# Chunked attention and a token/channel mixer on one core: x of one block put by in DRAM, a gate on seven parts, three additions without priority

## The chip, the cores and the metric

The kernel runs on one core of a Trainium2 chip. The metric is the device time of one execution in microseconds (us); the time before is the median of three runs. A profile comes from one further execution, and its times count from the start of that execution's span.

## The reference

Four batches of 768 tokens. A local attention with 8 heads of 64 dimensions gives x (768 x 512 per batch); a mixer adds a low-rank product over the tokens and then a two-layer network over the channels (512 to 2048 to 512).

```python
for c in range(768 // 32):                    # chunks of 32 queries
    k_full = concat(mem_k, k[16 before the chunk .. 8 after it])
    v_full = concat(mem_v, v[the same rows])
    a = softmax(q_c @ k_full.T / 8)
    out[:, :, 32 * c:32 * c + 32] = a @ v_full
x = out as (batch, 768, 512)
u = x + (x.transpose(0, 2, 1) @ U @ V).transpose(0, 2, 1)
result = u + relu(u @ w_ch1) @ w_ch2          # all in float32 accuracy
```

The weights U, V, w_ch1 and w_ch2 arrive as float64 words and are decoded in the kernel.

## The kernel before

To keep float32 accuracy, each float32 operand is split into a high part (fp32r) and a low part, and a product is made of three passes of TensorE (PE): high by high, high by low, low by high. Tokens are worked in blocks of 384 (TB = 3 tiles of 128, so two blocks per batch), hidden channels in 16 factors f of 128 (NF).

**Stages.** `attention(0)` runs first. Then `both_blocks` works off batch 0 in 32 units, numbered n: units 0 to 17 alternate between block 0 and block 1 over f = 0 to 8 while the weights are still being decoded, units 18 to 24 finish block 0 (f = 9 to 15), units 25 to 31 finish block 1. A unit is a `w1_step` (12 matmuls into a bank of PSUM, then ReLU: hh on ACT, hl on VectorE, DVE) and later a `w2_step` (9 matmuls into three accumulator banks). During the last units batch 1's attention is woven in. The attention result x of a token tile is a 128 x 512 tile in SBUF, kept in `xs` in one of 19 equal slots (pool `tk`) until the sums of w2 are added to it in `add_to_x` (L1174). `put_by` hands x to a list, `let_go` issues the listed stores on ACT's queue (or, when told, on SP's), and `recall` gets new slots and loads x back from DRAM on SP's queue.

**The seam.** Batches 1 to 3 use a seven-product scheme (Strassen-like) in place of eight products. For that, three calls of `fold_both` (L1379 to L1399), one for each of the last units of batch 0, transpose x of batch 1 and make seven combinations of it, held as th (high, cast by ACT, L1393) and tl (low, subtracted by DVE, L1394), each with parts 0 to 6. One fold writes its parts in four pieces: 5 and 6, 0 and 1, 2 and 3, and part 4; the planner runs them in the order in which their inputs come, part 4 second. Then `seven` runs `products(p)` for each pair p of factors: seven products of six matmuls (L1459) on three banks; product 0 uses part 6, product 1 part 2, product 2 part 0. After each product, DVE or ACT combines banks (L1465 to L1478).

GpSimd builds five weight sums per pair in `prepare` (L1346). Before those of pair 1, a one-element copy into `gate_` (L1334) reads part 4 of tl at the last token: GpSimd works in program order, so nothing of its later work runs before that element is written.

**What sets the order.** SP, PE and GpSimd follow the program's order. ACT (from unit 2 on) and DVE (from unit 18 on) follow an order that a planner makes ahead of time from its own estimates: it takes the ready instruction of the highest priority. Priority is program order, and `tc.high_priority(offset=...)` lifts an instruction by so many places; HIGH is 400. The fold is lifted by HIGH, so are the combinations in `products`, and the last additions to x by 2 x HIGH.

Of the kernel before, what the change touches and what calls it, by code (L numbers as in the profile page):

```python
# [9 lines left out]
F32 = mybir.dt.float32  # L10
# [26 lines left out]
HIGH = 400  # L37
LEAD = 0
LATE = 0
SPLIT = 9  # L40
# [15 lines left out]
def chunk_attn_then_mixer_kernel(  # L56
# [13 lines left out]
    nc = tc.nc  # L70
    ctx.enter_context(tc.manual_schedule(engines={mybir.EngineType.SP}))
    P = 128
# [16 lines left out]
    TB = 3  # L89
    NBLK = NT // TB  # L90
    TOK = TB * P
# [3 lines left out]
    const = ctx.enter_context(tc.tile_pool(name="const", bufs=1))  # L95
# [13 lines left out]
    def slot(shape, dtype, name):  # L109
        return tk.tile(shape, dtype, name=name, tag="slot")  # L110
# [58 lines left out]
    for j in range(4):  # L169
        nc.gpsimd.tensor_copy(  # L170
            out=rep[32 * j:32 * j + 32],
            in_=ident[32 * j:32 * j + 32, None, 32 * j:32 * j + 32].broadcast_to([32, 3, 32]),
# [242 lines left out]
    def advance(n):  # L415
        for _ in range(n):
            next(weights, None)
# [652 lines left out]
    def more_w():  # L1070
        while loaded[0] < min(NF, done[0] // 2 + EARLY):
            if loaded[0] >= 5 and front[0]:
                return
            if loaded[0] >= LASTF - NDEC and done[0] < ndec[0]:
                return
            load_w(loaded[0])
            loaded[0] += 1
# [26 lines left out]
    rest, gate = [], []  # L1104

    def turn_x1(c):

        ps = att_ps()
        for tt in range(TB):
            nc.tensor.matmul(  # L1110
                out=ps[:, tt * P:(tt + 1) * P], lhsT=xs[(0, TB + tt)][:, c * P:(c + 1) * P],
                rhs=ident, start=(tt == 0), stop=False, is_transpose=True, skip_group_check=True,
            )
        return ps
# [8 lines left out]
    def join_uT1(ps, c, g3):  # L1123
        if (0, 1) not in uT:
            u_pair(0, 1)
        uh, ul = (a[c] for a in uT[(0, 1)])
        nc.tensor.matmul(
            out=ps[:, 0:TOK], lhsT=g3[:, c * P:(c + 1) * P], rhs=v3[:, TOK:2 * TOK],
            start=False, stop=True, skip_group_check=True,
        )  # L1130
        nc.scalar.copy(out=uh, in_=ps[:, 0:TOK])  # L1131
        nc.vector.tensor_tensor(out=ul, in0=ps[:, 0:TOK], in1=uh.bitcast(F32), op=ALU.subtract)
# [5 lines left out]
    def put_by(b, t):  # L1138
        held.append((x_d[b, t], xs.pop((b, t))))

    def let_go(eng=nc.scalar):
        while held:
            to, x = held.pop(0)
            eng.dma_start(out=to, in_=x)

    def recall(b, blk):
        for t in range(blk * TB, blk * TB + TB):
            x = xs[b, t] = slot([P, CH], F32, "x")
            nc.sync.dma_start(out=x, in_=x_d[b, t])
# [20 lines left out]

    def add_to_x(b, t, bank, last):
        x = xs[(b, t)]
        with tc.high_priority(offset=2 * HIGH if last else 0):
            nc.vector.tensor_tensor(out=x, in0=bank, in1=x, op=ALU.add)  # L1174
        if last:
            held.append((out[b, t * P:(t + 1) * P, :], xs.pop((b, t))))
            if b == B - 1 or b == 0 and t >= TB:
                let_go(nc.sync)
        else:
            put_by(b, t)  # L1180
# [42 lines left out]
    def get_w1l(f):  # L1223
        if f not in w1ls:
            w1ls[f] = fetch_w1l(f)

    def both_blocks(following):

        units = []
        for f in range(SPLIT + LEAD):  # L1230
            if f < SPLIT:
                units.append((0, f, 0, f == 0, None))
            if f >= LEAD:
                g = f - LEAD
                units.append((1, g, 1, g == 0, False if g == SPLIT - 1 else None))
        units += [(0, f, 0, False, True if f == NF - 1 else None) for f in range(SPLIT, NF)]
        units += [(1, f, 0, f == SPLIT, True if f == NF - 1 else None) for f in range(SPLIT, NF)]
        prev = []
        for n, (blk, f, where, begins, ends) in enumerate(units):
            while done[0] < min(2 * NF, 2 * f + 1 + (n > LATE)):  # L1240
                advance(1)
                more_w()
            if n == 2:
                head.close()
            let_go()
            solo = n >= 2 * SPLIT
            if n == 2 * SPLIT:
                paced.close()
            for blk_, m, *_ in units[n:n + AHEAD + 1]:
                if m >= SPLIT and blk_ == 1:  # L1250
                    get_w1l(m)
            w1l = w1ls[f]
            if f >= SPLIT or blk == 1:
                del w1ls[f]
            if n == 2 * SPLIT - SOON:
                place(1)
            serve(RATEL if n < 2 * SPLIT else RATES)
            if n > 2 * SPLIT:
                border()
            if n == 0:  # L1260
                for c, g3 in rest[:2]:
                    join_uT1(turn_x1(c), c, g3)
            if n == len(units) - 1:
                for m in range(3):
                    build_factor(0, m)
            hid_ = w1_step(0, blk, f, w1l)
            if n == len(units) - 5:
                open_turned()
            if n == len(units) - 1:
                open_fast()  # L1270
            if n == 0:
                decode(2, 4)
                for c, g3 in rest[2:]:
                    join_uT1(turn_x1(c), c, g3)
                decode(1, 1)
                decode(2, 6)
                decode(1, 6)
                decode(3, 2)
            for _ in range(RATE + (3 < n < 12)):
                advance(1)  # L1280
                more_w()
            if n > 2 * SPLIT:
                border()
            if n == len(units) - 3:
                prepare(0, True)
            if n >= len(units) - 3:
                following()
            if n == len(units) - 1:
                recall(0, 1)
                for m in (3, 4):  # L1290
                    build_factor(0, m)
            prev.append((blk, f, where, begins, ends) + hid_)
            if solo or n % 2 == 0 or ends:
                while len(prev) > (not ends):
                    while done[0] < 2 * prev[0][1] + 2:
                        advance(1)
                        more_w()
                    w2_step(0, *prev.pop(0))

    def place(n):  # L1300
        for _ in range(n):
            next(gen[0], None)

    def serve(n):
        for _ in range(n):
            if next(feed[0], "shut") == "shut":
                return
# [10 lines left out]
    def border():  # L1318
        run_tails()
        place(PLAN[at[0]])  # L1320
        at[0] += 1

    gate_ = const.tile([P, 1], F32, name="gate")
    sums_d = [[dram.tile([P, 2, 2, P], F32, name=f"sumsd{p}_{m}") for m in range(3)] for p in range(NF // 2)]

    def prepare(p, first):

        if first:
            whole = [slot([P, NCK, P], F32, "val") for _ in range(2)]
            for side in range(2):  # L1330
                nc.gpsimd.dma_start(out=whole[side], in_=val_d[2 * p + side])
            mixed[p, 1], mixed[p, 3] = whole[1][:, 2:4, :], whole[0][:, 0:2, :]
            if p == 1:
                nc.gpsimd.tensor_copy(out=gate_[0:1], in_=turned[0][1][0:1, 4, 0, TOK - 1:TOK].bitcast(F32))  # L1334
        else:
            plain = slot([P, 2, 2, P], F32, "plain")
        for m, (n, fa, ca, fb, cb, op) in enumerate(SUMS):
            if m % 2 == 0:
                two = slot([P, 2, 2, P], F32, "sums")
                used = slice(0, 1 if m + 1 == len(SUMS) else 2)  # L1340
                if not first:
                    nc.sync.dma_start(out=two[:, used], in_=sums_d[p][m // 2][:, used])
            mixed[p, n] = two[:, m % 2]
            if first:
                a, b_ = (whole[f][:, 2 * c:2 * c + 2, :] for f, c in ((fa, ca), (fb, cb)))
                nc.gpsimd.tensor_tensor(out=two[:, m % 2], in0=a, in1=b_, op=getattr(ALU, op))  # L1346
                if m % 2 == 1 or m + 1 == len(SUMS):
                    summed.append((p, sums_d[p][m // 2][:, used], two[:, used]))
            elif m == 0:
                for n, side in ((1, 1), (3, 0)):  # L1350
                    mixed[p, n] = plain[:, side]
                    nc.sync.dma_start(out=plain[:, side], in_=val_d[2 * p + side][:, 2 * side:2 * side + 2])
# [9 lines left out]
    turned = [None]  # L1362
# [234 lines left out]
```

## Time and profile before

| | us |
|---|---|
| median of three runs | 647.34 |
| the three runs | 647.22, 647.34, 649.98 |
| the profiled execution | 647.76 |
| its span, first to last instruction | 646.0 |
| TensorE busy in the span | 626.6 (97%) |
| VectorE busy | 422.4 (65%) |
| ScalarE busy | 306.6 (47%) |
| GpSimd busy | 75.0 (12%) |

PE, DVE, ACT, POOL and SP are TensorE, VectorE, ScalarE, GpSimd and SyncE. Matmuls are pipelined and overlap in the records, so PE's progress is read from starts, not from sums of durations. A wait is put down to the instruction whose signal came last. A DMA issue is shown at the engine whose queue issues it (ACTq, SPq); where the queue stands, everything behind it in that engine's program stands too.

### The profile page before, as it was taken

The numbers are of one execution on the slowest core, as the hardware profiler recorded it, in microseconds if no ns is written. First come the engines' busy times: TensorE is split into PE (matmuls) and PEld (weight loads), VectorE is DVE, ScalarE is ACT, GpSimd is POOL, SyncE is SP. The second block draws the span as 40 slices with busy tenths as digits, with TensorE's granted clock in tenths as the row PEclk, the third lists the DMA queues.
The fourth block names the chain that finished last, engine by engine and source line by source line (L and its number), as shares of the span: only waits on it lengthen the run. The fifth ranks groups of instructions, "written<-read, shape, count | busy, mean of one in ns | idle before, by whom it ended". The sixth has DMA issues, their size and how long they took to land.

```text
span 646.0 us, 15746 instructions
## 1 busy us (share of the span) xinstructions
PE 626.6 (97%) x6196; PEld 548.8 (85%) x6198; DVE 422.4 (65%) x889; ACT 306.6 (47%) x770; POOL 75.0 (12%) x129
## 2 busy tenths in 40 slices
PE   7798999999999999989999999999999999999997
PEld 6567999988879899879898899888888899889986
DVE  4977997887529867449676864556666974427442
ACT  4666776685316454524344555633333653315320
POOL 3710011100120642123300000000000000000000
PEclk9999999999999999989999999999999999999999
DMA  9998695696606689414371699144532662100021
GB/s 206 192 306 294 212 261 180 181 255 177 185 22 220 183 219 208 132 35 157 100 236 52 170 208 230 43 116 124 148 114 82 189 221 90 50 34 16 2 79 69
DMA packets 134357, 96.83 MB, mean 150 GB/s; under 512 B 88842, under 2 KB 111114, under 8 KB 134282
## 3 DMA queue, kind: packets, MB, share of 16 engines
q1 hardware_dynamic: 121690, 70.25, 41.2%
q10 hardware_dynamic: 9936, 17.04, 7.2%
q0 software_dynamic: 2656, 8.52, 3.8%
q8 instruction: 49, 0.80, 0.5%
q14 instruction: 26, 0.21, 0.1%
HBM read 69.44 MB, written 25.43 MB: 147 GB/s over the span
## 4 chain that ended last, share of the span: by engine, by line
PE 88%; DVE 4%; SPq 2%; ACT 2%; DMA 2%; issue 1%; DVEq 0%; ACTq 0%
PE ps_h L1459 19%; PE acc L1213 14%; PE ps_h L1159 10%; PE ps_a L1459 8%; PE acc L1218 7%; PE ps_h L1213 6%; PE ps_a L1213 5%; PE ps_h L1218 3%; PE ps_a L582 2%; PE ps_a L1218 2%; PE ps_a L790 2%; PE ps_a L661 2%; PE ps_h L1205 1%; PE ps_a L760 1%; PE ps_a L1379 1%
## 5 line engine op out<-in xcount | busy, mean ns | idle before, releaser
L1213 PE MATMUL acc<-w,hh 128*128 128x512 f32 x366 | 97.1, 400 | 0.9 <-DVE w L367 0.9
L1459 PE MATMUL ps_h<-th,w1l 128*128 128x384 f32 x288 | 83.3, 342 | 0.5 <-DVE part L1474 0.5
L1213 PEld LDWEIGHTS acc<-w,hh 128*128 128x128 f32 x366 | 66.9, 188 | 15.2 <-issue 1.5
L1435 DVE SCALAR_TENSOR_TENSOR hl<-kept,hh 128x384 fp32r<-128x384 f32 x48 | 26.7, 556 | 50.9 <-PE ps_a L1218 25.7
L1459 PEld LDWEIGHTS ps_h<-th,w1l 128*128 128x128 f32 x288 | 52.8, 187 | 3.7 <-issue 1.7
L1434 ACT ACTIVATE hh<-kept 128x384 fp32r<-128x384 f32 x48 | 25.5, 531 | 64.0 <-PE ps_a L1213 41.5
L1459 PE MATMUL ps_h<-th,s 128*128 128x384 f32 x192 | 53.0, 337 | 0.0
L1218 PE MATMUL acc<-w,hl 128*128 128x512 f32 x183 | 51.6, 390 | 0.0
L1459 PE MATMUL ps_h<-tl,w1l 128*128 128x384 f32 x144 | 48.5, 337 | 0.0
L1213 PE MATMUL ps_h<-w,hh 128*128 128x512 f32 x156 | 43.9, 404 | 1.8 <-issue 1.8
L1159 PE MATMUL ps_h<-uh,w1h 128*128 128x384 f32 x124 | 42.5, 348 | 0.7 <-ACT uh L1131 0.6
L1159 PE MATMUL ps_h<-ul,w1h 128*128 128x384 f32 x124 | 40.9, 337 | 0.0
L1218 PEld LDWEIGHTS acc<-w,hl 128*128 128x128 f32 x183 | 34.4, 188 | 7.4
L1213 PE MATMUL ps_a<-w,hh 128*128 128x512 f32 x132 | 38.1, 392 | 1.7 <-ACT hh L1165 1.7
L1465 ACT COPY part<-ps_h 128x384 f32<-128x384 f32 x24 | 11.5, 479 | 55.5 <-PE ps_h L1459 34.5
L1427 ACT CAST s<-sums 128x256 fp32r<-128x256 f32 x72 | 28.6, 411 | 16.3 <-PE ps_h L1459 16.1
L1213 PEld LDWEIGHTS ps_h<-w,hh 128*128 128x128 f32 x156 | 29.0, 192 | 7.8 <-issue 1.9
L1459 PEld LDWEIGHTS ps_h<-th,s 128*128 128x128 f32 x192 | 35.1, 188 | 0.2 <-DVE part L1469 0.2
L1346 POOL TENSOR_TENSOR sums<-val 128x256 f32<-128x256 f32 x40 | 31.9, 825 | 28.1 <-DMA val<-vald 11.0
L1459 PE MATMUL ps_h<-tl,s 128*128 128x384 f32 x96 | 32.3, 337 | 0.0
L1213 PEld LDWEIGHTS ps_a<-w,hh 128*128 128x128 f32 x132 | 25.0, 190 | 7.5 <-ACT hh L1165 2.2
L1428 DVE TENSOR_TENSOR s<-sums,s 128x256 fp32r<-128x256 f32 x72 | 30.4, 434 | 1.0 <-ACT s L1427 0.8
(280 smaller groups left out, 1393.8 us busy)
## 6 DMA issues: line engine op xcount, KB each, us to landing
sums<-sumsd SPq DMA_DIRECT2D x32, 256.0 KB
xd<-x ACTq DMA_DIRECT2D x30, 256.0 KB
x<-xd SPq DMA_DIRECT2D x30, 256.0 KB
rw<-in_moe_w_ch_dram SPq DMA_DIRECT2D x14, 512.0 KB
vb<-in_v_dram SPq DMA_DIRECT2D x56, 98.0 KB
raw<-in_moe_w_ch_dram SPq DMA_DIRECT2D x20, 256.0 KB
qn<-in_q_dram SPq DMA_DIRECT2D x36, 128.0 KB
rw<-in_moe_w_ch_dram SPq DMA_DIRECT2D x16, 256.0 KB
```

Of the source, the lines that this page charges most:

```text
L582: nc.tensor.transpose(out=psv[:, p, r, :], in_=half[:, r, 2 * p:2 * p + 2, :].rearrange("n h d -> n (h d)"), identity=ident,)
L661: nc.tensor.matmul(out=psv[s][CK * i:CK * i + CK, t, p % 2, p // 2, :], lhsT=qt[p // 2][rows, p % 2, NI * t + i, :], rhs=kall[rows, NB * ( ...
L790: nc.tensor.matmul(out=psv[g][CK * i:CK * i + CK, t, j], lhsT=pt[j % 2][rows, 2 * t + j // 2, CK * i:CK * i + CK], rhs=vt[rows, NI * t + i ...
L1159: nc.tensor.matmul(out=ph[:, :TOK], lhsT=w[:, c, :], rhs=u[c], start=(m == 0), stop=(m + 1 == len(parts)),)
L1213: nc.tensor.matmul(out=acc[tt], lhsT=h[:, sl], rhs=w, start=(begins and m == 0), stop=False,)
L1218: nc.tensor.matmul(out=acc[tt], lhsT=hl[:, sl], rhs=w2h[f], start=False, stop=ends is not None)
L1346: nc.gpsimd.tensor_tensor(out=two[:, m % 2], in0=a, in1=b_, op=getattr(ALU, op))
L1427: nc.scalar.copy(out=s[:, 0:2], in_=total)
L1428: nc.vector.tensor_tensor(out=s[:, 2:4], in0=total, in1=s[:, 0:2].bitcast(F32), op=ALU.subtract)
L1434: nc.scalar.activation(out=hh, in_=src, func=AF.Relu)
L1435: nc.vector.scalar_tensor_tensor(out=hl, in0=src, scalar=0.0, in1=hh.bitcast(F32), op0=ALU.max, op1=ALU.subtract,)
L1459: nc.tensor.matmul(out=banks[at_], lhsT=w[:, wc, :], rhs=t[:, i, c, :], start=(n < 3 and m == 0), stop=(m + 1 == len(parts)), skip_group_c ...
```

## The change

At unit 2 of `both_blocks` the three x tiles of batch 0's block 0 are put by: stored to DRAM on ACT's queue and their slots given back. At unit 21 (2 x SPLIT + 3, SPLIT = 9) they are recalled on SP's queue into three new slots; the additions to them come after unit 24. The gate copies one element of each of tl's seven parts, not of part 4 alone. The last additions of batch 0's block 1 (t of 3 and more) keep the place that the program gives them; the other last additions keep their lift of 2 x HIGH.

```diff
     def add_to_x(b, t, bank, last):
         x = xs[(b, t)]
-        with tc.high_priority(offset=2 * HIGH if last else 0):
+        with tc.high_priority(offset=2 * HIGH if last and (b > 0 or t < TB) else 0):
             nc.vector.tensor_tensor(out=x, in0=bank, in1=x, op=ALU.add)
...
             if n == 2:
                 head.close()
+                for t in range(TB):
+                    put_by(0, t)
+            if n == 2 * SPLIT + 3:
+                recall(0, 0)
             let_go()
...
-    gate_ = const.tile([P, 1], F32, name="gate")
+    gate_ = const.tile([P, 7], F32, name="gate")
...
             if p == 1:
-                nc.gpsimd.tensor_copy(out=gate_[0:1], in_=turned[0][1][0:1, 4, 0, TOK - 1:TOK].bitcast(F32))
+                nc.gpsimd.tensor_copy(out=gate_[0:1], in_=turned[0][1][0:1, :, 0, TOK - 1].bitcast(F32))
```

## Rows read from the trace of the kernel before

**Rows 1.** Waits of PE, 50 to 216 us: us in total, times, longest.

```profile
PE ps_a L1213 <- ACT hh L1165: 1.7, 1, 1.7
PE ps_a L661 <- issue: 1.1, 1, 1.1
PE ps_a L1459 <- DVE tl L1394: 1.0, 1, 1.0
PE acc L1213 <- DVE w L367: 0.9, 1, 0.9
```

**Rows 2.** Timeline of PE at the seam: start us, us, operation [idle before].

```profile
213.56 0.34 PE L1459 MATMUL ps_a<-th,w1l 128*128 128x384 f32 x1
214.91 0.44 PE L1459 MATMUL ps_a<-tl,w1l 128*128 128x384 f32 x1 [1.02 <-DVE tl L1394]
...
215.90 0.34 PE L1459 MATMUL ps_h<-th,w1l 128*128 128x384 f32 x1
```

**Rows 3.** Windows, two pairs: us, busy of each engine, clock, DMA.

```profile
212.49:221.26 8.77, 7.75 (x44) 7.29 (x42) 7.94 (x15) 3.64 (x10) 6.46 (x10) 1.00 0.65 212
221.26:228.58 7.32, 7.32 (x43) 7.29 (x43) 4.50 (x11) 2.28 (x5) 5.53 (x9) 1.00 0.79 169
```

**Rows 4.** Timeline of DVE at the seam, columns as in group 2.

```profile
211.63 1.02 DVE L1394 TENSOR_TENSOR tl<-fold,th 128x512 fp32r<-128x512 f32 x2
212.56 1.28 DVE L1174 TENSOR_TENSOR x<-acc,x 128x512 f32<-128x512 f32 x2
213.76 2.23 DVE L1394 TENSOR_TENSOR tl<-fold,th 128x512 fp32r<-128x512 f32 x2
215.92 0.68 DVE L1174 TENSOR_TENSOR x<-acc,x 128x512 f32<-128x512 f32 x1
```

**Rows 5.** Timeline of GpSimd (POOL) at the seam.

```profile
212.71 0.18 POOL L1334 COPY gate<-tl 1x1 f32<-1x1 f32 x1 [7.77 <-DVE tl L1394]
212.89 4.63 POOL L1346 TENSOR_TENSOR sums<-val 128x256 f32<-128x256 f32 x5
```

**Rows 6.** DVE's groups by form, 199 to 208 us: busy us, mean ns, idle.

```profile
L1394 DVE TENSOR_TENSOR tl<-fold,th 128x512 fp32r<-128x512 f32 x6 | 3.9, 686 | 0.0
```

**Rows 7.** DVE's groups by form, 212.6 to 217 us.

```profile
L1394 DVE TENSOR_TENSOR tl<-fold,th 128x512 fp32r<-128x512 f32 x2 | 2.2, 1155 | 0.0
L1174 DVE TENSOR_TENSOR x<-acc,x 128x512 f32<-128x512 f32 x3 | 2.0, 681 | 0.0
...
L1428 DVE TENSOR_TENSOR w1l<-sums,w1l 128x256 fp32r<-128x256 f32 x1 | 0.4, 409 | 0.0
```

**Rows 8.** Timelines of SP, DVE and PE behind the seam.

```profile
217.05 0.39 SPq L488 DMA_DIRECT2D kn<-in_k_dram  x1
...
221.22 0.38 SPq L491 DMA_DIRECT2D kn<-in_k_dram  x1
...
227.22 0.56 DVE L1435 SCALAR_TENSOR_TENSOR hl<-ps_a,hh 128x384 fp32r<-128x384 f32 x1 [2.06 <-ACT hh L1434]
...
228.58 1.04 PE L582 MATMUL ps_a<-ident,kn 128*128 128x128 f32 x8
```

**Rows 9.** DMA issues, 40 to 235 us: KB, median us to landing.

```profile
val<-vald POOLq DMA_DIRECT2D x8, 256.0 KB, 4.1
```

**Rows 10.** Window around PE's third wait, columns as in group 3.

```profile
130.00:140.00 10.00, 8.93 (x69) 7.75 (x67) 8.62 (x17) 10.00 (x36) 0.00 (x0) 1.00 1.12 294
```

**Rows 11.** Waits of ACT, whole span, columns as in group 1.

```profile
ACT part L1465 <- DMA xd<-x: 17.6, 4, 4.7
```

**Rows 12.** Timelines of DVE and PE beside the new stores.

```profile
62.89 0.69 DVE L367 TENSOR_TENSOR w1l<-vbe,w1h 128x512 fp32r<-128x512 f32 x1
...
64.57 0.87 PE L1159 MATMUL ps_h<-uh,w1l 128*128 128x384 f32 x4
```

**Rows 13.** Timelines of DVE and PE at block 0's last additions.

```profile
167.75 1.89 DVE L1174 TENSOR_TENSOR x<-acc,x 128x512 f32<-128x512 f32 x3 [3.18 <-PE acc L1218]
...
175.93 1.42 PE L1213 MATMUL acc<-w,hh 128*128 128x512 f32 x5
```

## The prediction

> **What bounds the kernel now.** TensorE (PE) does, nearly everywhere, so I looked for the moments at which it stands still. The first view is the list of PE's waits over the part of the span that the change touches, from 50 to 216 us. It names four, 4.7 us together [rows 1]: 1.7 us on ACT's hh, 0.9 us on a low half of w2, 1.1 us that the profile puts down to "issue", and 1.0 us on a DVE subtraction of the fold (tl, L1394). That sum caps what the three edits can give back here. The second view is PE's timeline around 212 us, the seam at which batch 0 ends and batch 1's seven-product scheme begins. Product 1's first matmul starts at 213.56, its second waits 1.02 us for tl, and product 2 starts only at 215.90 [rows 2]. The third view prices the seam as a whole: the first pair of factors takes 8.77 us, the next pair, with the same 42 matmuls, 7.32 us at the same granted clock of 1.00 [rows 3]. The reader is to see that the seam loses 8.77 - 7.32 = 1.45 us, more than the 1.02 us that the wait names, because PE also runs unevenly as it resumes.
>
> The fourth view says why. On DVE, two of the last fold's four tl subtractions run from 211.63, then two additions L1174 of batch 0's result (212.56, 1.28 us for both), then the other two tl from 213.76, which take 2.23 us, then the third addition at 215.92 [rows 4]. GpSimd opens its gate at 212.71, when part 4 of tl is written but parts 0 to 3 are not, and starts its five sums at 212.89 [rows 5]. A tl of this shape takes 686 ns in the two folds before, where GpSimd adds nothing, and 1155 ns here [rows 6, 7]. So PE's wait has two causes: two additions stand ahead of the tl that it needs, and that tl is slow beside GpSimd.
>
> **The change part by part.** *Additions without priority, gate on all parts.* These remove the wait together. Without the 2 x HIGH lift, the three additions rank behind the fold, which keeps its own lift of HIGH. Then the third tl (parts 2 and 3) starts at 212.56, where the first addition stood, and runs 0.69 us, since the gate is shut: it ends at 213.25. In the two folds before, DVE had no idle time ahead of any tl [rows 6], so ACT's casts should not hold it up. PE needs these parts with product 1's second matmul, one matmul interval (1.05 us / 6 = 0.17 us; 7.32 / 7 = 1.05 us per product [rows 3]) after 213.56: at 213.73. That is 0.48 us of room. The fourth tl (parts 0 and 1) ends by 213.25 + 0.69 = 213.94, and PE wants it in product 2, from 213.56 + 1.05 = 214.61. Product 1 shrinks from 215.90 - 213.56 = 2.34 us to 1.05 us, a gain of 1.29 us [rows 2, 3]; the other 0.16 us of the 1.45 is the uneven resumption, which I expect mostly to go too.
>
> What is late next? The additions now start near 213.9 and, at 0.68 us each [rows 7], end near 216.0, against 216.60 before [rows 4]: no later for SP, whose stores of the result wait for them and hold batch 2's loads of k behind them. They could delay the combination L1467, which product 4 needs at 212.49 + 4 x 1.05 = 216.69. L1467 can start when product 1 is done (214.61); if all three additions go first it ends near 216.0 + 0.55 = 216.55. The cost is nothing, by 0.1 us, and at most some tenths.
>
> The gate is a wait, so what is queued behind it on GpSimd counts: five sums for pair 1, two memsets, and the loads of pair 2's values. All start about 1.2 us later than now (213.94 against 212.7). Pair 1's first sum is needed by product 0 of that pair, at 221.26 - 1.45 = 219.8; sums that begin at 214.2 and take 4.63 us for all five [rows 5] end at 218.8. So their delay is covered by the seven products of pair 0. Uncovered, it would cost up to 1.2 us.
>
> The slowdown does not vanish with the gate: it moves to whatever DVE runs beside the sums. The rows show that it spares what would stand there: the additions took 681 ns beside GpSimd, and an L1428 of w1l 409 ns [rows 7]. The Trainium skill (SBUF — State Buffer, "Who interferes with whom") says that a DVE instruction with two SBUF inputs contends with a GpSimd instruction that reads SBUF, and that whoever issues first holds the port pair for the whole instruction. The tl's 686 against 1155 ns agrees; the L1428 at 409 ns, also with two SBUF inputs, shows no cost. By the rule each later L1428 could still wait out a sum.
>
> *x of block 0 to DRAM and back.* It adds three stores on ACT's queue at unit 2 and three loads on SP at unit 21, and frees three of the 19 slots in between. No PE wait between them names a slot or a load, so I book no gain. The cost: the stores' issue can hold ACT, which is in order. The trace has no such store at that place; its bounds are nothing (hidden in idle time) and 4.7 us, the longest hold of ACT by a DMA in this kernel [rows 11]. The tightest work behind is factor 2's low half: DVE writes it at 62.89 + 0.69 = 63.58, and PE wants it at 64.57, so 1.0 us of hold is free [rows 12] and the bounds on the time are 0 and 3.7 us. I take 0, since ACT's waits between 44 and 216 us name no DMA. SP's three loads are needed by the additions that begin at 167.75 and last 1.89 us; PE uses those banks again at 175.93 [rows 13], so the loads may be 6.3 us late before PE notices. Slots are no scarcer after unit 21 than before the change. I book 0 there, too.
>
> **Sum.** -1.29 - 0.16 + 0 = -1.4 us. The profiled run took 647.76 us for a span of 646.0, so 1.76 us lies around the span and stays. It becomes 646.4; taken from the median of 647.34, 645.9 us.
>
> **The rivals.**
>
> *The stall shrinks but stays, or moves.* If the planner, which orders DVE by its own estimates, finds tl not ready when PE's last sums are, it still puts two additions first. Then the closed gate alone helps: tl runs from 213.76 to 214.45 and PE resumes some 0.7 us late instead of 1.3. Or L1467 and the L1428 copies queue up behind additions and sums, by the port rule above. Either gives back 0.4 to 0.9 us of the 1.45: about 646.7. For it: DVE is busy 7.94 of 8.77 us there [rows 3]. Against: the rows of the additions and of L1428 show no slowdown [rows 7].
>
> *A second wait goes, too.* The 1.1 us wait at the first scores of batch 1 [rows 1] falls into a stretch in which ACT is 10.00 of 10 us busy [rows 10]; so it is probably ACT's copy of q, late in its queue. With other slots, the planner may order that stretch otherwise: 645.9 - 1.1 = 644.8. Nothing in the change aims at it.
>
> *Slower: the stores hold ACT at unit 2.* Place: ACT's queue ahead of the casts of factors 1 and 2. It decides from a hold of 1.0 us on; at 4.7 us it costs 3.7 us [rows 11, 12], so 645.9 + 3.7 = 649.6, above the time before. Against: all other ACT waits in this stretch are for DVE or PE.
>
> *Slower still: the additions slide.* With no lift at all they rank behind everything that products raises by HIGH. If the third ran only in DVE's next long gap, 2.06 us ahead of 227.22, SP's loads of k for batch 2 would start there instead of at 217.05. The last of the first group is issued at 221.22 + 0.38 and would land, at the 4.1 us of a 256 KB load, at 225.7; PE transposes at 228.58, or 227.1 after the gain [rows 8, 9]. So the additions may end 1.4 us later than 216.60; each us beyond costs PE one. An end near 224 gives 645.9 + 6 = 652. Against: DVE has nothing else to do at 213.9.
>
> **How the numbers follow.** Forecast 645.9 (own range 645.6 to 646.4): 0.57. Shrunken or moved stall, 646.7: 0.20. Second wait, 644.8: 0.10. Stores hold ACT, up to 649.6: 0.07. Additions slide, about 652: 0.06. The range takes the first three and the lower half of the fourth, with some tenths for the spread of medians: 644.4 to 648.4. A difference below 0.5% (3.2 us) can't be told from no change by such a measurement. Faster than 644.1 would need more waits than the rows name near the edits: 0.04. Slower than 650.6 takes the last rival: 0.06. Same: 0.90.
>
> **What would show it.** In the changed kernel's trace the four tl of the last fold stand in one row near 2.2 us with no addition among them, the gate follows the last of them, the additions come next, and the wait of product 1 for L1394 is gone; the first pair of factors takes about 7.4 us. GpSimd's sums start near 214.2, relative to the seam. Stores and loads of x appear near unit 2 and unit 21 with no new wait of PE. I am wrong if the first pair still takes over 8 us, if a wait for L1467, L1469 or kn replaces the old one, or if a stretch before 205 us has grown.

## The result, and the profile after

The changed kernel is slower, not faster: 651.72 us median of 19 runs (651.1 to 655.63), beside 648.46 us (646.13 to 652.54, 19 runs) for the kernel before in the same session. The ratio is 1.0053 with a 95% interval of 1.0036 to 1.0071. The forecast was 645.9 us, with a range that ended at 648.4. The profiled execution took 652.4 us with a span of 650.6 us, 4.6 us longer than the 646.0 us before.

Where it went is seen best if the start of one and the same matmul is read in both traces (of each kernel one execution):

| matmul of PE | before, us | after, us | later by |
|---|---|---|---|
| scores L661 of batch 0, the group at 25.58 us | 25.58 | 32.28 | 6.70 |
| join of the low-rank product, L1095 | 42.03 | 49.37 | 7.34 |
| a w1 unit, L1159 | 61.38 | 70.09 | 8.71 |
| product 1, second matmul | 214.91 | 223.16 | 8.25 |
| scores of batch 2, L661 | 274.47 | 282.56 | 8.09 |
| w2 step behind the scores of batch 2, L1213 | 277.74 | 284.45 | 6.71 |
| the same stretch, L1213 | 282.28 | 287.55 | 5.27 |
| end of the span | 646.0 | 650.6 | 4.6 |

So the loss is made before 33 us, ahead of every stretch that the prediction looked at. At the seam the change gains, but some 0.5 us instead of 1.45. Between 274 and 283 us the profiled execution of before lost 2.8 us (8.09 - 5.27) that this one did not; that stretch is taken up again below.

The 6.70 us are not all the change's. The profiled execution of before is early in the front part: the kernels below that have no hold there start this L661 group at 26.92 to 28.91 us, 1.3 to 3.3 us behind it, and those with the hold at 32.28 to 32.93. At the first w1 matmul of the unit near 61 us, the start is 61.03 in before, 62.25 to 64.54 in the six kernels without the hold, and 68.53 to 69.45 in the three with it. Between the middles of the last two groups, 62.81 and 68.89, lie some 6 us; that is my estimate of what the hold costs PE by there.

**The loss.** The longest of PE's waits of the changed kernel from 0 to 45 us (total, times, longest); it was 0.6 us before. Behind it the L661 group, in the changed kernel and then in the one before:

```profile
PE ps_a L661 <- ACT qt L642: 6.4, 2, 6.2
...
32.28 2.23 PE L661 MATMUL ps_a<-kall,qt 64*32 64x64 f32 x127 [6.23 <-ACT qt L642]
```

```profile
25.58 1.81 PE L661 MATMUL ps_a<-kall,qt 64*32 64x64 f32 x128
```

ACT's timeline there says why the copies of q (qt, L642) are late:

```profile
25.66 0.44 ACT L216 ACTIVATE dec<-vraw 96x256 f32<-96x256 f32 x1 [0.65 <-DMA vb<-in_v_dram]
31.46 0.34 ACTq L1144 DMA_DIRECT2D xd<-x  x1
31.84 0.39 ACT L642 COPY qt<-ps_h 128x256 f32<-128x256 f32 x1 [5.75 <-DMA vbe<-in_v_dram]
31.94 0.36 ACTq L1144 DMA_DIRECT2D xd<-x  x1
32.11 0.68 ACT L642 COPY qt<-ps_h 128x256 f32<-128x256 f32 x2
```

In the kernel before the same place reads:

```profile
24.74 0.45 ACT L216 ACTIVATE dec<-vraw 96x256 f32<-96x256 f32 x1 [0.79 <-DMA vraw<-in_moe_V_dram]
25.09 1.21 ACT L642 COPY qt<-ps_h 128x256 f32<-128x256 f32 x4
```

The store of x (L1144) belongs to unit 2, which runs after 60 us, but x is ready near 25 us, and the planner has put the store into ACT's queue at once, between the decay factors and the q copies. There ACT stands for 5.75 us, the store's own issue of 0.34 us included. It doesn't wait for x: the bracket names a load of v. In the kernel as built this store carries two waits, one for VectorE and one for a completion counter (number 0 of eight that the DMAs of SP and ACT take in turn); the transfer that used that counter last is this load of v. No run gives the store another counter, so this step rests on the built kernel and the trace. The chain of waits shows when the load came (start us, us, what):

```profile
18.59 6.01 DMA uarea<-in_moe_U_dram
24.60 0.02 issue
24.61 0.61 SPq L563
...
27.04 0.41 SPq L563
...
27.49 0.45 SPq L563
...
27.98 3.41 DMA vbe<-in_v_dram
...
31.41 0.02 ACTq L1144
```

SP's queue was issuing one load after another, and it had itself stood 1.1 us, to 24.60, for an earlier load (uarea); the turn of this load of v came at 27.98, after ACT had already stopped at its store, and it landed 3.41 us later. The Trainium skill (DMA: Bandwidth & Descriptors, "Issuing engines are not separate DMA queues") says that issuing from several engines saves only the time of initiating, which is usually small beside the transfer. One issue of 0.41 to 0.45 us beside the 3.41 us from issue to landing agrees. Ahead of this load stands a row of eight issues that took 5.30 us on the one queue, the stand of 1.1 us among them; so the row, not the single issue, made it late.

While PE stood, its granted clock fell. Windows of the changed kernel, and below them one of the kernel before (us, busy of PE, PEld, DVE, ACT, POOL, granted clock, DMA share, GB/s):

```profile
25.00:30.00 5.00, 1.05 (x10) 0.81 (x8) 2.01 (x7) 0.44 (x2) 0.77 (x2) 0.92 0.87 185
30.00:35.00 5.00, 2.72 (x174) 2.66 (x174) 0.66 (x2) 2.77 (x8) 0.24 (x1) 0.50 0.85 224
35.00:40.00 5.00, 2.99 (x115) 2.06 (x101) 4.60 (x15) 1.26 (x2) 3.28 (x7) 0.89 0.12 34
...
65.00:70.00 5.00, 3.95 (x11) 3.21 (x12) 3.90 (x7) 3.70 (x9) 0.00 (x0) 0.68 0.61 210
```

```profile
30.00:35.00 5.00, 5.00 (x106) 3.12 (x102) 4.70 (x16) 3.19 (x7) 2.96 (x6) 0.66 0.65 148
```

A clock of 0.50 is the level of 1.2 GHz. The L661 group took 2.23 us there (32.28, 127 matmuls) against 1.81 us in before (25.58, 128). The last row of the changed kernel is a second dip, in which the lag grows from 7.34 to 8.71 us; the kernel with the stores alone, below, has the hold but a clock of 1.00 in that window, so I don't count this step to the change.

**The seam.** DVE, GpSimd and PE of the changed kernel, beside [rows 2, 4, 5]:

```profile
220.28 1.02 DVE L1398 TENSOR_TENSOR tl<-fold,th 128x512 fp32r<-128x512 f32 x2
221.22 1.28 DVE L1174 TENSOR_TENSOR x<-acc,x 128x512 f32<-128x512 f32 x2
222.41 1.29 DVE L1398 TENSOR_TENSOR tl<-fold,th 128x512 fp32r<-128x512 f32 x2
223.62 0.69 DVE L1174 TENSOR_TENSOR x<-acc,x 128x512 f32<-128x512 f32 x1
...
223.77 0.18 POOL L1338 COPY gate<-tl 1x7 f32<-1x7 f32 x1 [10.17 <-DVE tl L1398]
...
223.16 0.45 PE L1463 MATMUL ps_a<-tl,w1l 128*128 128x384 f32 x1 [0.60 <-DVE tl L1398]
```

The two additions still stand ahead of the tl that PE needs: the order of [rows 4] is unchanged. The gate now opens after the last tl, and with GpSimd silent these two tl take 1.29 us instead of 2.23. PE's wait for them falls from 1.02 to 0.60 us, and the first pair of factors takes 8.24 us instead of the 8.77 of [rows 3]:

```profile
221.15:229.39 8.24, 7.64 (x43) 7.31 (x42) 7.70 (x14) 3.89 (x11) 5.42 (x10) 1.00 0.64 207
```

The slowdown beside GpSimd has not gone; it has moved to the low halves of the factors, which took 408 to 457 ns behind the seam in before, where the sums were done or nearly so (DVE's groups by form, 223.8 to 229.4 us: busy us, mean ns):

```profile
L1432 DVE TENSOR_TENSOR w1l<-sums,w1l 128x256 fp32r<-128x256 f32 x2 | 1.5, 733 | 0.2 <-ACT w1l L1431 0.2
L1432 DVE TENSOR_TENSOR w1l<-val,w1l 128x256 fp32r<-128x256 f32 x2 | 1.4, 722 | 0.0
```

No wait of PE follows from that here.

### The profile page after: what moved, and what is told of

It reads as the page before. It is cut to its first block, busy times and chain, and to the rows that moved or that the text cites. A ratio compares the mean times of both kernels' runs of the same rounds, so it can differ in the third digit from the quotient of the medians.

```text
span 650.6 us, 15769 instructions
## 1 busy us (share of the span) xinstructions
PE 625.1 (96%) x6198; PEld 548.5 (84%) x6198; DVE 420.7 (65%) x889; ACT 306.1 (47%) x770; POOL 74.4 (11%) x129
## 4 chain that ended last, share of the span: by engine, by line
PE 86%; DMA 4%; DVE 3%; SPq 3%; ACT 1%; issue 1%; ACTq 0%; DVEq 0%
PE ps_h L1463 19%; PE acc L1213 14%; PE ps_h L1159 10%; PE ps_a L1463 7%; PE acc L1218 7%; PE ps_h L1213 6%; PE ps_a L1213 5%; PE ps_h L1218 3%; PE ps_a L1218 3%; PE ps_a L582 2%; DMA rw<-in_moe_w_ch_dram 2%; PE ps_a L661 2%; PE ps_a L790 2%; SPq L563 1%; PE ps_h L1205 1%
## 5 line engine op out<-in xcount | busy, mean ns | idle before, releaser
L1213 PE MATMUL acc<-w,hh 128*128 128x512 f32 x366 | 97.1, 400 | 1.0 <-DVE w L367 1.0
L1213 PEld LDWEIGHTS acc<-w,hh 128*128 128x128 f32 x366 | 66.9, 188 | 15.1 <-issue 1.5
L1213 PE MATMUL ps_h<-w,hh 128*128 128x512 f32 x156 | 43.0, 398 | 0.4 <-issue 0.4
L1159 PE MATMUL ps_h<-uh,w1h 128*128 128x384 f32 x124 | 42.6, 349 | 0.8 <-ACT uh L1131 0.8
L1159 PE MATMUL ps_h<-ul,w1h 128*128 128x384 f32 x124 | 41.1, 339 | 0.0
L1213 PE MATMUL ps_a<-w,hh 128*128 128x512 f32 x132 | 38.6, 396 | 1.7 <-ACT hh L1165 1.7
L1469 ACT COPY part<-ps_h 128x384 f32<-128x384 f32 x24 | 11.5, 479 | 55.7 <-PE ps_h L1463 39.3
L1213 PEld LDWEIGHTS ps_h<-w,hh 128*128 128x128 f32 x156 | 28.4, 188 | 6.2 <-issue 0.6
L1471 DVE TENSOR_TENSOR part<-ps_a,part 128x384 f32<-128x384 f32 x24 | 13.3, 555 | 28.6 <-PE ps_a L1463 26.3
L1213 PEld LDWEIGHTS ps_a<-w,hh 128*128 128x128 f32 x132 | 25.0, 190 | 7.4 <-ACT hh L1165 2.2
```

The costliest lines, as they stand in the source:

```text
L1159: nc.tensor.matmul(out=ph[:, :TOK], lhsT=w[:, c, :], rhs=u[c], start=(m == 0), stop=(m + 1 == len(parts)),)
L1213: nc.tensor.matmul(out=acc[tt], lhsT=h[:, sl], rhs=w, start=(begins and m == 0), stop=False,)
L1471: nc.vector.tensor_tensor(out=ta, in0=b2, in1=ta, op=ALU.subtract)
```

## The experiments

The theory from these rows: the loss is the hold of ACT by the first store, at the place that the planner chose. The rivals: the bytes of six added transfers cost time wherever they run; or the seam, with gate and priority, loses it. The kernels below are the changed kernel with the edit shown, and each is compared with the kernel before in five rounds of the same session.

### The stores and the recall alone

```diff
-        with tc.high_priority(offset=2 * HIGH if last and (b > 0 or t < TB) else 0):
+        with tc.high_priority(offset=2 * HIGH if last else 0):
...
-    gate_ = const.tile([P, 7], F32, name="gate")
+    gate_ = const.tile([P, 1], F32, name="gate")
...
-                nc.gpsimd.tensor_copy(out=gate_[0:1], in_=turned[0][1][0:1, :, 0, TOK - 1].bitcast(F32))
+                nc.gpsimd.tensor_copy(out=gate_[0:1], in_=turned[0][1][0:1, 4, 0, TOK - 1:TOK].bitcast(F32))
```

> The change without its gate and its priority: only the stores of block 0's x at unit 2 and their recall. Hold theory (the planner puts the first store on ACT ahead of the copies of q in batch 0's attention, where it stands 5.75 us for a load of v): all of the loss is here, so 3.3 to 4.5 us above the kernel before, the 6.2 us wait of PE for L642 near 26 us stays, and the seam wait of 1.0 us for tl is back. Rival, seam theory (the gate or the slide of the additions costs): equal to the kernel before within 1 us, no wait of PE above 2 us before 45 us.

Measured: 654.91 us (653.02 to 656.74, 6 runs), ratio 1.0093 [1.0058, 1.0129]. ACT's wait and PE's two waits of interest:

```profile
31.98 0.38 ACT L642 COPY qt<-ps_h 128x256 f32<-128x256 f32 x1 [5.90 <-DMA vbe<-in_v_dram]
...
PE ps_a L661 <- ACT qt L642: 6.8, 2, 6.4
...
PE ps_a L1463 <- DVE tl L1398: 1.0, 1, 1.0
```

The hold is there, and the wait at the seam is back at 1.0 us. The loss comes with the stores. It is larger than I had expected: 6.3 us by the medians, against 3.3 to 4.5. The changed kernel loses 3.3 us in its own session; the gain at the seam explains some 0.5 us of that difference, the two intervals overlap, and the rest stays open.

### The gate and the priority alone

```diff
             if n == 2:
                 head.close()
-                for t in range(TB):
-                    put_by(0, t)
-            if n == 2 * SPLIT + 3:
-                recall(0, 0)
```

> The change without the stores and the recall: only the gate on seven parts and the additions without priority. Hold theory: nothing of the loss, 0.4 to 1.0 us below the kernel before, PE's wait for tl at the seam 0.6 us instead of 1.0, no new wait before 45 us. Seam theory: 3 us or more above the kernel before.

Measured: 646.1 us (644.75 to 651.77, 12 runs) beside 648.62, ratio 0.9968 [0.9943, 0.9993]. This beats both kernels. At the seam:

```profile
213.94 1.01 DVE L1394 TENSOR_TENSOR tl<-fold,th 128x512 fp32r<-128x512 f32 x2
214.88 1.28 DVE L1174 TENSOR_TENSOR x<-acc,x 128x512 f32<-128x512 f32 x2
216.08 1.28 DVE L1394 TENSOR_TENSOR tl<-fold,th 128x512 fp32r<-128x512 f32 x2
...
214.81:222.99 8.18, 7.58 (x44) 7.26 (x43) 7.70 (x14) 3.88 (x11) 5.38 (x10) 1.00 0.64 207
```

The pair takes 8.18 us, 0.59 us less than in [rows 3]. The medians differ by 2.5 us, more than the 0.4 to 1.0 that I had expected; what lies beyond the 0.59 us is open (see the next section).

### The gate alone

```diff
-        with tc.high_priority(offset=2 * HIGH if last and (b > 0 or t < TB) else 0):
+        with tc.high_priority(offset=2 * HIGH if last else 0):
...
-                for t in range(TB):
-                    put_by(0, t)
-            if n == 2 * SPLIT + 3:
-                recall(0, 0)
```

> GpSimd's gate waits for all seven parts of tl; no stores, and the priority of the last additions as in before. VectorE's order near the end of the fold is that of before: tl, tl, addition, addition, tl, tl, addition. If GpSimd's sums beside tl are what the change gained at the seam, the gate alone gives it: the last two tl take 1.28 us in place of 2.23, TensorE's wait for tl falls from 1.0 to 0.6 us, the shift there is -0.4 to -0.5 us, and the time is before -0.4 to -0.6 (the stretch at 276 to 283 us can give up to 1.3 more). If the priority made it, the wait stays at 1.0 and the time at that of before.

Measured: 646.87 us (645.74 to 650.36, 12 runs) beside 648.05, ratio 0.9981 [0.9961, 1.0001]. The two tl again take 1.28 us behind two additions, and PE waits 0.60 us:

```profile
215.85 0.45 PE L1459 MATMUL ps_a<-tl,w1l 128*128 128x384 f32 x1 [0.60 <-DVE tl L1394]
```

As built, this kernel has, on each of the five engines, the same instructions with the same waits in the same order as the kernel of gate and priority above. Likewise, a kernel with the priority edit alone is, instruction for instruction, the kernel before. So the priority edit does nothing at all, and the gain at the seam is the gate's. The two sections thus time one and the same program twice, 2.5 us and 1.2 us below the kernel before: part of the 2.5 us is spread of the medians, and the interval of the second just reaches 1.

### The whole change, stores issued by SP

```diff
                 for t in range(TB):
                     put_by(0, t)
+                let_go(nc.sync)
```

> The whole change, but the three stores are issued on SP, which follows the program's order, at unit 2. Hold theory: ACT meets no store early, PE's 6.2 us wait is gone, the time is 0.5 us below the kernel before to 0.5 above. Traffic rival (768 KB more to move while weights and v stream in, whichever engine issues them): still 2 to 4 us above the kernel before, with waits of ACT or DVE for loads between 45 and 75 us.

Measured: 647.41 us (645.24 to 650.79, 12 runs) beside 648.62, ratio 0.998 [0.9955, 1.0004]. SP follows the program's order, so the stores stay at unit 2:

```profile
L1144 SPq DMA_DIRECT2D xd<-x x3: 319/320/343, 53.9 to 56.1; - x3
```

Of PE's waits for L642 0.2 us are left. The same bytes, stored and recalled at the place that the program names, cost nothing that can be measured beside the kernel before: the rival of the traffic, with 2 to 4 us, falls. Beside gate and priority alone, in the same session, the median is 1.3 us longer, and the intervals overlap.

### The whole change, stores by ACT in the program's order

```diff
             if n == 2:
-                head.close()
                 for t in range(TB):
                     put_by(0, t)
+                let_go()
+                head.close()
```

> The whole change, but put_by and the stores stand ahead of head.close, so ACT still follows the program's order and the stores come behind unit 1's casts. Hold theory: no hold near 26 us; at their new place the stores wait for loads already under way, up to 1.4 us each by SP's waits there, of which about 1 us is free: 0.5 us below the kernel before to 2 us above. Traffic rival: 2 to 4 us above, as in the kernel with the stores on SP.

Measured: 650.53 us (647.67 to 653.92, 12 runs) beside 648.62, ratio 1.0024 [0.9999, 1.0048]. The stores now stand at 64 us, behind a cast of w, and hold nothing there; PE doesn't wait for qt at 26 us. What is left comes from elsewhere. Waits of PE, and ACT's timeline at the longer one:

```profile
PE ps_a L661 <- issue: 5.1, 2, 3.6
...
142.43 0.71 ACT L391 CAST w2last<-vb 128x512 fp32r<-128x512 f32 x1
142.94 0.53 ACT L216 ACTIVATE dec<-rw 128x256 f32<-128x256 f32 x1
143.27 0.77 ACT L642 COPY qt<-ps_a 128x256 f32<-128x256 f32 x2
```

PE's L661 starts at 143.85, behind these q copies. In before the wait at this place is the 1.1 us of [rows 1], and the copies ran at 139.26. So "issue" most likely stood for ACT's copy of q, late in a full queue, as the prediction guessed; here the planner has set the cast of w1h, which ran behind the copy in before, ahead of it. From 145 to 150 us PE then ran at a granted clock of 0.72. I count both as an effect of the planner's new order; no run separates it further.

### One store of three: tile 0, or tile 2

```diff
-                for t in range(TB):
+                for t in (0,):
                     put_by(0, t)
             if n == 2 * SPLIT + 3:
-                recall(0, 0)
+                for t in (0,):
+                    x = xs[0, t] = slot([P, CH], F32, "x")
+                    nc.sync.dma_start(out=x, in_=x_d[0, t])
```

Gate and priority are as in the kernel before; the second kernel has (2,) for (0,).

> Only tile 0 of the three is stored to DRAM and fetched back; GpSimd's gate and the priority of the last additions are as in the kernel before. ACT's order in this kernel still has the store directly behind the last decay factor of L216 and ahead of the q copies of L642. If the loss is the hold of the first store in ACT's queue, this one store costs nearly what three do: TensorE's L661 waits about 6 us for qt of L642 near 25.5 to 32 us, the shift at the first L661 is +5.5 to +6.5 us, and the time is 4 to 6 us above before (some 651 to 654). If the loss grows with the number of stores or their bytes, it is a third: 1.5 to 2.5 us above before. The wait for tl at the seam stays at 1.0 us in both.

> Only tile 2 is stored and fetched back; gate and priority as in the kernel before. In ACT's order this store stands later, behind L704 and ahead of L265, where the changed kernel had its third store at 39.9 us. If the place of the store and the transfer that its wait names make the loss, there is no hold at 26 us, L661 starts at 25.6 as in before, and the time is before +0 to +1.4 us. If stores cost by their number or bytes, it equals the kernel with tile 0 alone: +1.5 to +2.5 us.

Measured, beside 648.05: tile 0 alone 654.06 us (652.4 to 656.5, 6 runs), ratio 1.0083 [1.0057, 1.0109]; tile 2 alone 648.45 us (646.88 to 651.36, 12 runs), ratio 1.0005 [0.9983, 1.0027]. ACT with tile 0 alone, and then with tile 2 alone:

```profile
32.12 0.33 ACTq L1144 DMA_DIRECT2D xd<-x  x1
32.49 0.66 ACT L642 COPY qt<-ps_h 128x256 f32<-128x256 f32 x2 [5.53 <-DMA vbe<-in_v_dram]
```

```profile
26.50 1.20 ACT L642 COPY qt<-ps_h 128x256 f32<-128x256 f32 x4
...
35.36 0.42 ACTq L1144 DMA_DIRECT2D xd<-x  x1
35.82 0.37 ACT L265 CAST v<-ps_a 96x256 fp32r<-96x256 f32 x1 [2.29 <-DMA vbe<-in_v_dram]
```

One store ahead of the q copies costs as much as three (6.0 us of medians, against 6.3). PE's own wait there is 4.3 us instead of the 6 that I had expected, because PE came later to the place; its L661 starts at 32.93, beside 32.28 in the changed kernel. One store behind them costs nothing that can be measured, although it, too, stands 2.29 us for a load of v: there PE doesn't wait for what is queued behind. So it is the place and the wait, not the number of stores.

### All four tl ahead of the additions

```diff
+            if n == len(units) - 1:
+                paced.enter_context(tc.manual_schedule(engines=PACED))
             if n >= len(units) - 3:
                 following()
...
                     w2_step(0, *prev.pop(0))
+        paced.close()
```

The stores are left out; VectorE keeps the program's order through the last unit.

> Gate and priority as in the change, no stores, and VectorE's work of the last unit in the order of the program, so that all four tl stand ahead of the three additions. My theory of the seam: what is left of TensorE's wait for tl there (0.6 us) is the two additions of L1174 between the tl, 1.28 us. With them behind, tl ends near 1.3 us sooner than with gate and priority alone, the wait of 0.6 us is gone, TensorE's shift behind the seam is -1.0 to -1.2 us instead of -0.5, and the time is 0.4 to 0.7 us below that of gate and priority alone (some 645.5 beside before at 648). Rival: the wait is replaced by one for another operand (th of the same fold, or w1l, whose subtractions on VectorE also change places), and the shift stays near -0.5 us. A rival on the slow side: the subtractions for the factors, now behind the fold and the additions, hold TensorE at the fourth product, a wait for w1l or s of 0.5 us or more.

Measured: 648.33 us (646.95 to 651.44, 12 runs) beside 648.05, ratio 1.0001 [0.9983, 1.002]. The tl end sooner, and the wait for them is gone; another stands 5.6 us behind its place:

```profile
214.38 1.63 DVE L1397 TENSOR_TENSOR tl<-fold,th 128x512 fp32r<-128x512 f32 x3 [0.28 <-ACT th L1396]
...
216.59 1.88 DVE L1174 TENSOR_TENSOR x<-acc,x 128x512 f32<-128x512 f32 x3
218.39 0.54 DVE L1470 TENSOR_TENSOR part<-ps_a,part 128x384 f32<-128x384 f32 x1
218.86 0.79 DVE L1431 TENSOR_TENSOR w1l<-sums,w1l 128x256 fp32r<-128x256 f32 x1
219.57 0.95 DVE L1431 TENSOR_TENSOR w1l<-val,w1l 128x256 fp32r<-128x256 f32 x1
...
220.78 0.54 DVE L1472 TENSOR_TENSOR part<-ps_h,part 128x384 f32<-128x384 f32 x1
...
221.38 0.44 PE L1462 MATMUL ps_h<-th,s 128*128 128x384 f32 x1 [1.07 <-DVE part L1472]
...
214.46:223.57 9.11, 8.04 (x43) 7.22 (x42) 9.11 (x19) 3.57 (x9) 5.81 (x10) 1.00 0.62 193
```

The first rival of the prediction, that the stall moves, came true: VectorE is busy for 9.11 of 9.11 us in this pair, the additions and two w1l slowed by the sums stand ahead of the combination L1472 (L1469 in the kernel before), and product 5, which adds onto the bank that this combination reads, waits 1.07 us for it. The pair takes 9.11 us, longer than in before. My theory of the seam, that the two additions are what is left to take away, falls.

## Why the prediction was wrong

**The step that failed** is the booking of the stores: "I take 0, since ACT's waits between 44 and 216 us name no DMA". Three things in it were wrong. *The place.* I put the stores "at unit 2", where the program has them, though I had written myself that the planner takes the ready instruction of the highest priority. That a store stands at unit 2 in the program doesn't keep it there: x is ready near 25 us, and the planner let the store go ahead of the q copies. The row to read was not [rows 12], near 63 us, but ACT's queue from the moment at which x is ready; the list of ACT's waits that the 0 rests on begins at 44 us. *The free time.* I gave the store 1.0 us of cover from [rows 12]; at its real place the q copies are wanted at once, and there is none. *The size.* I had 4.7 us as the longest hold [rows 11]. The hold was 5.75 us, and PE's L661 came 6.70 us later than in the early trace of before, 3.4 to 5.4 us later than in the kernels without the hold. The rival "the stores hold ACT at unit 2" had 0.07, with the right mechanism (an in-order queue stands at a DMA issue) and the wrong place; it gave "up to 649.6".

**The recall** was right: no new wait of PE near unit 21, and with SP's stores the whole change is at the level of before.

**The seam** was mis-sized: 8.77 - 8.24 = 0.53 us instead of 1.45. The step that failed is "the three additions rank behind the fold". They do, and it changes nothing: as built, the order is that of before. My reading, which no row shows, is that by the planner's estimates the tl are not ready when the additions are. That was the rival "the stall shrinks but stays", with 0.4 to 0.9 us, and it is what happened; the kernels of gate and priority confirm it. The next term was mis-sized, too: "The cost is nothing, by 0.1 us" counts the additions ahead of L1467, but not the low halves w1l that follow it, which only the first rival names; with the tl ahead, it is the wait for L1469 behind them that costs 1.07 us.

**The gate** did as said: GpSimd's later start held up nothing on PE. But "it spares what would stand there" was wrong. It rested on one L1428 of 409 ns [rows 7]; of four beside the sums, two took near 0.5 us and two near 0.95, 722 to 733 ns in the mean. The rule of the Trainium skill (SBUF — State Buffer, "Who interferes with whom"), that a VectorE instruction with two SBUF inputs contends with a GpSimd instruction that reads SBUF, was the better guide. The traces agree with it: 733 against 408 ns, while the additions, with one input in PSUM, kept their 680 to 690 ns. In the kernel with the tl ahead this is part of the new wait.

**The size of the rest.** From 274 to 283 us the profile of before has 1.8 us of PE's "issue" wait and then slow matmuls, 2.8 us in all that the changed kernel doesn't lose. Before, then changed:

```profile
280.00:290.00 10.00, 10.00 (x48) 8.29 (x48) 3.19 (x6) 3.66 (x10) 1.60 (x3) 0.87 0.00 0
```

```profile
280.00:290.00 10.00, 9.59 (x168) 7.87 (x167) 6.69 (x11) 3.78 (x9) 3.84 (x6) 1.00 0.55 126
```

In seven other traces that wait is 0.2 to 1.3 us, with and without the stores (in the other two PE waits at L661 instead, 0.5 and 1.5 us), and in all nine the granted clock there is 1.00, so I don't count it to the change. It is why the two profiles differ by only 4.6 us, where the lag of 8.71 us less the seam's gain would leave some 8. The one profile of before was thus early in front and late here, which nearly cancels in its time; it is a poor yardstick for a single stretch, and the medians are the better one. What sets this wait stays open.

## What to carry to other kernels

A DMA issue given to an engine whose order a planner makes is placed by when its data is ready, not by where the program has it: look at that engine's queue from that moment on, and issue from a queue in program order where the place matters. An issue can also wait for the completion of another queue's transfer, one that has nothing to do with its data, if the two share a counter; price that by when the other transfer will be issued. Where a second engine is nearly full beside a stall (VectorE, 7.94 of 8.77 us here), reordering its work can only move the stall, as it did here; the part that went was gained by making that work faster. And read one stretch in several traces before pricing it: here the same matmul near 26 us started up to 3.3 us apart without any hold.

## What the runs showed of the hardware

In the changed kernel a stand of about 6 us of PE went with a granted clock of 0.50 in the window from 30 to 35 us, where the kernel before had 0.66, and the lag grew from 6.70 us at the L661 group to 7.34 us by 49 us; how much of that is the clock, no run separates. A dip alone is no sign of the hold: four kernels without it show 0.66 or 0.67 in the window from 25 to 30 us. The other unexpected number is the reach of GpSimd's sums: the slowdown of VectorE's subtractions (408 to 733 ns in the mean) moved with the sums to the instructions with two SBUF operands that ran beside them, and there to two of the four.
